# Unread float16 products among the first attention scores, and two groups of transfers written at other steps

## The chip, the cores and the metric

The kernel runs on one core of a Trainium2 chip. The metric is the device time of one execution in microseconds (us), taken as the median of several executions. Engines are named as in the profile: PE (TensorE) multiplies matrices, PEld is its weight load, DVE (VectorE) does elementwise work and reductions, ACT (ScalarE) evaluates functions and copies, POOL (GpSimd) works on the side, and SP (SyncE) starts nearly all transfers from one queue.

## The reference

Three layers run one after another on 3072 rows of 512 numbers.

- Attention: 4 batches, 8 heads, 768 positions, 64 numbers per head. A position sees the first `n_global` = 8 positions and the `n_local` = 96 positions up to itself, with a bias that falls with distance; then softmax and the product with `v`.
- A dense layer: `h = x @ w_in` (512 to 2048), `g = h if h > 0 else exp(h) - 1`, `y = g @ w_out` (2048 to 512).
- A routed layer: a row is kept as it is unless `x @ w_skip > 0`; the other rows go to the one of 8 experts with the largest gate logit, `out = x + gate * (relu(x @ w1[e]) @ w2[e])`.

```python
scores = scale * q @ k.T + bias; a = softmax(where(keep, scores, -1e9)); x = a @ v
h = x @ w_in; y = where(h > 0, h, exp(min(h, 0)) - 1) @ w_out
out[do_compute] = y + gate_w * (relu(y @ w1[e]) @ w2[e])
```

All inputs are float32. The kernel multiplies in float16 wherever it can, each operand split into a high and a low part, so that one product of the reference becomes three.

## The kernel before, in words

**Attention steps.** `att_step(t)` (line 350) handles one step: a tile `n` of 128 rows and one of its four pairs of heads. It issues the scores of step `t` (`att_scores`, line 239 on PE, line 248 on DVE, the exponential in line 253 on ACT), the preparation of the step before (`att_probs`, `att_turn`; line 293 is the transpose on PE) and the product with `v` of four steps back (`att_pv`, line 324). The first six tiles' scores, and everything of the first four tiles, are products of float32 operands; later tiles use float16 parts. Each pair of scores has one buffer per head (`s0`, `s1`), so the scores of a step wait until DVE has read those of the step before.

**Weights of the dense layer.** `w_load` (line 387) brings one sixteenth of both weight matrices (1 MB) into one of two buffers (`stage`). `w_prep` first gathers the number out of its bits in three passes over 1024 elements on DVE (lines 396, 397, 398), then splits it into float16 parts (line 404 on ACT, line 405 on DVE). `w_check` (line 416) reads the same 16 MB a second time, as tiles `wc`, and folds one word of each number into `andw`, for a test at the end whether the inputs suit the fast path.

**Dense steps.** `moe_h(m, f)` (line 428, 12 products of 384 columns, then lines 432 to 439 on ACT, DVE and POOL) and `moe_y(m, f)` (line 449, nine products of 512 columns), for eight blocks `m` of 384 rows and sixteen pieces `f`. The body of `program` first runs 16 attention steps (`4 * TB + LV`) with twelve halves of weight preparation between them, and then the 128 dense steps, with the remaining attention steps and, in block 0, the remaining weight preparation between them. `route_init` (line 453) loads the gate's weights and clears the table `xg` by 16 transfers of 257 KB out of one tile `zrow` (line 475); it stands at step 12 of block 0. The second reading starts at step 16 (`c = s_ - NF`). From the second block on, `route` sends the rows of the block before to their experts; the experts themselves follow at the end.

**What sets the order.** The order in which `program` issues instructions is not the order in which they stand on the engines. The framework schedules each engine's instructions by its own estimate of when they are ready, and lets an instruction that is ready early pass others. `pin` (line 72) takes an instruction out of that freedom: pinned instructions keep the order of the program among each other. Transfers started by SP stand in one queue in that scheduled order, and each waits there for what it needs while those behind it wait too. Two transfers into `stage` can be under way at once; the next one waits until a buffer has been read.

Of the kernel before, what the change touches and what calls it, by code (L numbers as in the profile page):

```python
# [9 lines left out]
F32 = DT.float32  # L10
# [9 lines left out]
P = 128  # L20
B, H, S, D = 4, 8, 768, 64
NT, DM, FF = 3072, 512, 2048
E, F2 = 8, 1024
NB = S // P
NTILE = NT // P
TB = 3
TN = TB * P
NM = NT // TN
NF = FF // P
ND = DM // P  # L30
CAP = 256
# [10 lines left out]
ROW = DM + 2  # L42
# [9 lines left out]
LP, LV = 1, 4  # L52
# [10 lines left out]
class Fast:  # L63
# [281 lines left out]
    def att_xturn(self):  # L345
        if self.xs:
            xT, xs = self.xs.pop(0)
            self.nc.sync.dma_start_transpose(xT, xs.rearrange("p s h d -> p (s h d)"))

    def att_step(self, t):  # L350

        n, hp = divmod(t, H // 2)
        last = 4 * NTILE
        if t < last:
            self.att_scores(t)
        if 0 <= t - LP < last:
            self.att_probs(t - LP)
        if 0 <= t - LV < last:
            g = t - LV
            m, c = divmod(g // 4, TB)  # L360
            if m not in self.xT:
                self.xT[m] = self.mp.tile([P, 2 * ND, TN], F16, tag="xT", name=f"xT_{m}", bufs=2)
            self.att_pv(g, self.xT[m], c * P)
        if n + 1 < NTILE:
            self.att_split(n + 1, hp)
        if hp != 3 or n >= NTILE:
            self.att_xturn()
        if 0 <= t - LP < last:
            self.att_turn(t - LP)
        if hp == 1 and n + 2 < NTILE:  # L370
            self.att_load(n + 2)
# [81 lines left out]
    def route_init(self):  # L453
        nc = self.nc
        self.wg = self.ct([P, ND, E + 1], F32, "wg")
        nc.sync.dma_start(self.wg[:, :, 0:E], self.a["moe2_w_gate"].rearrange("(c p) e -> p c e", p=P))
        nc.sync.dma_start(self.wg[:, :, E:E + 1], self.a["moe2_w_skip"].rearrange("(c p o) -> p c o", p=P, o=1))

        self.wgs = self.ct([P, ND, 2, E + 1], F16, "wgs")
        t = self.ct([P, ND, E + 1], F32, "wgt")  # L460
        nc.vector.tensor_scalar(t, self.wg, GS, None, ALU.mult)
        nc.vector.tensor_copy(self.wgs[:, :, 0, :], t)
        nc.vector.tensor_tensor(self.wgs[:, :, 1, :], t, self.wgs[:, :, 0, :], ALU.subtract)
        nc.vector.tensor_tensor(t, t, t, ALU.mult)
        self.wgm = self.ct([P, 2], F32, "wgm")
        nc.vector.tensor_reduce(out=self.wgm[:, 0:1], in_=t[:, :, 0:E], op=ALU.max, axis=AX.XY)
        nc.vector.tensor_reduce(out=self.wgm[:, 1:2], in_=t[:, :, E], op=ALU.max, axis=AX.X)
        self.esum = self.ct([P, TB], F32, "esum")
        nc.vector.memset(self.esum, 0.0)
        self.xg = self.dp.tile([E * CAP, ROW], F32, name="xg")  # L470
        z = self.mp.tile([P, ROW], F32, tag="yt", name="zrow", bufs=4)
        nc.gpsimd.memset(z[:, 0:DM + 1], 0.0)
        nc.gpsimd.memset(z[:, DM + 1:ROW], OOB)
        for n in range(E * CAP // P):
            nc.sync.dma_start(self.xg[n * P:(n + 1) * P, :], z)

    def route(self, m):

# [317 lines left out]
    def program(self, ep, wp, ap):  # L796
        tc, nc = self.tc, self.nc
        self.att_init(ap)
        self.counts()
        self.w_init(ep, wp)  # L800
        self.att_load(0, "q")
        self.consts()
        self.att_load(1, "q")
        self.w_load(0)
        self.att_load(0, "v")
        self.att_load(1, "v")
        self.w_load(1)
        self.gsum = self.ct([P, NM * NF], F32, "gsum")
        self.sqw = self.ct([P, 2], F32, "sqw")
        self.vf0 = self.raw[0]  # L810
        self.tables(ap)
        self.att_split(0, 1)
        done = [0]

        def whalf():
            if done[0] < 2 * NF:
                f, part = divmod(done[0], 2)
                self.w_prep(f, part)
                done[0] += 1
                if part == 0 and f + 2 < NF:  # L820
                    self.w_load(f + 2)

        t = 0
        while t < 4 * TB + LV:
            self.att_step(t)
            if t == 2:
                self.att_split(0, 3)
                self.maxsq(self.vf0[:, 0, :], self.sq[:, 2, 0:1])
            for _ in range(W_STEPS.count(t)):
                whalf()  # L830
            t += 1
        steps = [(m, f) for m in range(NM) for f in range(NF)]
        pend = []
        todo = [(e, k, j) for e in range(E) for k in range(8) for j in range(2)]
        self.nh, self.htags = 0, ("h",)

        def prep():
            if todo:
                e, k, j = todo.pop(0)
                if j == 0 and len(todo) > 4:  # L840
                    self.ex_load(*todo[3][0:2])
                self.ex_prep(e, k, j)

        for s_, (m, f) in enumerate(steps):
            if m < NM - 1:
                for _ in range(A_STEPS[min(m, 1)].count(f)):
                    self.att_step(t)
                    t += 1
            if m == NM - 1 and f == 0:
                ap.release()  # L850
                self.xp = tc.alloc_tile_pool(name="xp", bufs=2)
                self.esums = self.xp.tile([P, 32 * E], F32, tag="esums", name="esums", bufs=1)
                self.emax = self.xp.tile([P, 2 * E], F32, tag="emax", name="emax", bufs=1)
                nc.gpsimd.memset(self.esums, 0.0)
                for k in range(2):
                    self.ex_load(0, k)
            while done[0] < 2 * f + 2 and m == 0:
                whalf()
            self.moe_h(m, f)
            if m == NM - 1:  # L860
                for _ in range(EX_HALVES[f]):
                    prep()
            if m == 0:
                for _ in range(2):
                    whalf()
            if pend:
                pend.pop(0)()
            if m == NM - 1 and f in (11, 13):
                assert not pend
                for e in range(NX):  # L870
                    (self.ex_gather if f == 11 else self.ex_tokens)(e, 0)
            if s_ >= LAG:
                self.moe_y(*steps[s_ - LAG])
            if m == 0 and f == 12:
                self.route_init()
            c = s_ - NF
            if c == 0:
                self.w_load(0, "wc")
            if 0 < c <= 4 * NF and c % 2 == 0:
                self.w_check(*divmod(c // 2 - 1, 2))  # L880
            if f == LAG and m:
                pend = self.route(m - 1)
                pend.pop(0)()
        for k in range(LAG):
            self.moe_y(*steps[k - LAG])
        self.ex_tail(prep)
        wp.release()
        self.xp.release()
# [271 lines left out]
```

## Time and profile before

| | us |
|---|---|
| three timed executions | 887.74, 889.18, 889.23; median 889.18 |
| the profiled execution, timed | 886.45 |
| span of the profiled execution | 884.7 |
| PE busy / DVE busy / ACT busy | 825.5 / 608.3 / 535.7 |
| mean granted TensorE clock | 0.966 |

The span runs from the first to the last instruction. The granted clock is the share of 2.4 GHz that TensorE was given: 1.00 is 2.4 GHz, 0.50 is 1.2 GHz. A busy time of PE counts the modelled ends of pipelined products, so a busy PE is not one at its peak. In a list by time, a row gives the start, the time until the last of its instructions has ended, engine, line, what is written and read, and how many instructions; one float32 product is two instructions in the trace. What stands in brackets is idle time of the engine before the row, and what ended it.

### The profile page before, as it was taken

The numbers are of one execution on the slowest core, as the hardware profiler recorded it, in microseconds if no ns is written. First come the engines' busy times: TensorE is split into PE (matmuls) and PEld (weight loads), VectorE is DVE, ScalarE is ACT, GpSimd is POOL, SyncE is SP. The second block draws the span as 40 slices with busy tenths as digits, with TensorE's granted clock in tenths as the row PEclk, the third lists the DMA queues.
The fourth block names the chain that finished last, engine by engine and source line by source line (L and its number), as shares of the span: only waits on it lengthen the run. The fifth ranks groups of instructions, "written<-read, shape, count | busy, mean of one in ns | idle before, by whom it ended". The sixth has DMA issues, their size and how long they took to land.

```text
span 884.7 us, 17522 instructions
## 1 busy us (share of the span) xinstructions
PE 825.5 (93%) x6017; PEld 478.8 (54%) x6017; DVE 608.3 (69%) x2263; ACT 535.7 (61%) x1326; POOL 175.6 (20%) x201
## 2 busy tenths in 40 slices
PE   4999898989899999999999999999999889999895
PEld 2766444445455555555555555555554556766563
DVE  6876999768847756755764775672586967877532
ACT  4655677656667777777777677664665645655311
POOL 1000212211222322221232232223232111101010
PEclk9966999989899999999999999999999989999998
DMA  8878987999966536455544542531445778978510
GB/s 310 231 202 212 261 263 224 324 283 250 253 127 129 113 89 153 104 120 101 126 103 126 126 89 49 113 73 33 110 160 176 244 224 256 267 247 250 136 43 25
DMA packets 185394, 148.79 MB, mean 168 GB/s; under 512 B 152208, under 2 KB 154256, under 8 KB 181200
## 3 DMA queue, kind: packets, MB, share of 16 engines
q1 hardware_dynamic: 182096, 141.59, 61.6%
q0 software_dynamic: 3200, 5.99, 1.9%
q8 instruction: 49, 0.80, 0.4%
q14 instruction: 49, 0.40, 0.1%
HBM read 94.82 MB, written 21.08 MB: 131 GB/s over the span
## 4 chain that ended last, share of the span: by engine, by line
PE 63%; DVE 13%; issue 11%; DMA 10%; ACT 1%; POOL 1%; SPq 0%; POOLq 0%; DVEq 0%; ACTq 0%
PE h L428 23%; PE y L449 22%; PE s L239 6%; PE pv L324 6%; DMA out<-eres,ix 5%; PE eh L639 3%; PE eo L655 2%; DMA wc<-in_wf 2%; DVE wt L397 2%; DVE w L405 2%; DVE wt L398 1%; DVE p L248 1%; PE ptp L293 1%; DVE e L435 1%; DMA wr<-in_wf 1%
## 5 line engine op out<-in xcount | busy, mean ns | idle before, releaser
L428 PE MATMUL h<-xT,w 128*128 128x384 f16 x1536 | 277.3, 331 | 2.9 <-DVE e L435 2.8
L449 PE MATMUL y<-w,gs 128*128 128x512 f16 x1152 | 271.2, 379 | 2.6 <-ACT gs L438 1.8
L439 POOL TENSOR_TENSOR gs<-e,gs 128x384 f16<-128x384 f32 x128 | 127.3, 995 | 423.9 <-ACT gs L438 359.8
L428 PEld LDWEIGHTS <-w 128*128 128x128 f16 x1536 | 148.1, 99 | 106.7 <-issue 11.6
L449 PEld LDWEIGHTS <-gs 128*128 128x128 f16 x1152 | 109.9, 98 | 123.4 <-ACT gs L438 2.8
L435 DVE SCALAR_TENSOR_TENSOR e<-e,h 128x384 f32<-128x384 f32 x128 | 70.4, 551 | 80.2 <-ACT e L433 78.0
L438 ACT ACTIVATE gs<-e 128x384 f16<-128x384 f32 x128 | 66.8, 522 | 97.0 <-DVE e L435 96.4
L253 ACT ACTIVATE p<-p,st 128x232 f32<-128x232 f32 (+1 forms) x192 | 89.2, 465 | 43.4 <-DVE st L248 42.9
L639 PE MATMUL eh<-eyT,ew 128*128 128x128 f16 (+1 forms) x1152 | 101.8, 239 | 4.6 <-DMA eyT<-eyh 3.1
L655 PE MATMUL eo<-ew,ehs 128*128 128x512 f16 x384 | 100.7, 384 | 5.4 <-DVE ehs L643 5.4
L639 PEld LDWEIGHTS <-ew 128*128 128x128 f16 x1152 | 86.7, 99 | 30.8 <-issue 4.8
L603 DVE SCALAR_TENSOR_TENSOR ew<-er,ew 128x512 f16<-128x512 f32 x128 | 88.8, 712 | 9.9 <-ACT ew L602 8.9
L432 ACT ACTIVATE e<-h 128x384 f32<-128x384 f32 x128 | 61.3, 479 | 48.7 <-PE h L428 40.6
L641 ACT ACTIVATE ehs<-eh 128x128 f16<-128x128 f32 (+1 forms) x96 | 29.9, 312 | 95.9 <-PE eh L639 92.8
L248 DVE CUSTOM_DVE_ANT_0 p<-s,tab 128x232 f32<-128x232 f32 (+1 forms) x192 | 67.1, 376 | 26.9 <-PE s L239 25.3
L602 ACT ACTIVATE ew<-er 128x512 f16<-128x512 f32 x128 | 75.4, 619 | 4.2 <-DMA er<-in_moe_w 4.1
L283 DVE TENSOR_TENSOR ph<-p,ph 128x464 f16<-128x464 f32 x68 | 43.5, 653 | 36.5 <-ACT ph L282 36.5
L433 ACT ACTIVATE e<-e 128x384 f32<-128x384 f32 x128 | 66.5, 520 | 3.1
L239 PE MATMUL s<-qh 64*128 64x232 f16 (+1 forms) x432 | 40.7, 258 | 14.5 <-DVE st L248 14.0
L655 PEld LDWEIGHTS <-ehs 128*128 128x128 f16 x384 | 35.1, 99 | 31.3 <-DVE ehs L643 8.3
L643 DVE SCALAR_TENSOR_TENSOR ehs<-eh,ehs 128x128 f16<-128x128 f32 (+1 forms) x96 | 31.7, 331 | 25.8 <-ACT ehs L641 25.5
L239 PE MATMUL s<-qk 64*128 64x232 f32 (+1 forms) x96 | 31.0, 565 | 15.6 <-DVE st L248 8.0
(170 smaller groups left out, 913.4 us busy)
## 6 DMA issues: line engine op xcount, KB each, us to landing
er<-in_moe_w SPq DMA_DIRECT2D x64, 512.0 KB
wr<-in_wf SPq DMA_DIRECT2D x16, 1024.0 KB
wc<-in_wf SPq DMA_DIRECT2D x16, 1024.0 KB
qk<-in_qk SPq DMA_DIRECT2D x20, 720.0 KB
out<-yt SPq DMA_DIRECT2D x24, 256.0 KB
rawv<-in_vp SPq DMA_DIRECT2D x21, 256.0 KB
xg<-zrow SPq DMA_DIRECT2D x16, 257.0 KB
yg<-xg SPq DMA_DIRECT2D x16, 257.0 KB
```

What stands on the lines that cost most here:

```text
L239: nc.tensor.matmul(sp[j], q[r, hp, KW:], k[r, hp, KW - w:KW], start=(x == 0), stop=(x == len(mm) - 1))
L248: nc.vector.tensor_tensor_reduce(pw[:, j, :], sp[j], self.tab[:, h, :] if i else self.tab0[:, h, :], -0.125, 3e38, ALU.add, ALU.min, st[:, ...
L253: nc.scalar.activation(pw[:, j, :], pw[:, j, :], AF.Exp, bias=st[:, 0, h:h + 1], scale=-1.0, accum_out=st[:, 1, h:h + 1])
L428: nc.tensor.matmul(hps, wi[:, s_, c, :], xT[:, x * ND + c, :], start=(n == 0), stop=(n == 3 * ND - 1))
L435: nc.vector.scalar_tensor_tensor(g, e, -HS, hps, ALU.mult, ALU.max, accum_out=self.gsum[:, m * NF + f:m * NF + f + 1])
L438: nc.scalar.activation(gs[:, 0], g, AF.Copy)
L439: nc.gpsimd.tensor_tensor(gs[:, 1], g, gs[:, 0], ALU.subtract)
L449: nc.tensor.matmul(self.ys[m][t], gs[:, s_, t * P:(t + 1) * P], wo[:, x, :], start=(f == 0 and n == 0), stop=(f == NF - 1 and n == 2))
L602: self.pin(nc.scalar.activation(w[:, 0], r, AF.Copy, scale=sc))
L603: nc.vector.scalar_tensor_tensor(w[:, 1], r, sc, w[:, 0], ALU.mult, ALU.subtract, accum_out=self.esums[:, c:c + 1])
L639: nc.tensor.matmul(hps, l, r, start=(i == 0), stop=(i == len(mm) - 1))
L655: nc.tensor.matmul(self.eo[(e, t)], hs[:, s_, j * P:(j + 1) * P], self.ew[(e, 4 + f // 2, f % 2)][:, x, :], start=(f == 0 and n == 0), sto ...
```

## The change: products on PE, and two groups of transfers

The change adds products whose result nobody reads, `keep_warm`: 40 ahead of step 0 and 8 ahead of each of the steps 1 to 15, 160 in all, each 128 x 128 times 128 x 256 in float16 on the constant tile `tri`, pinned. They write tiles of the tag `acc`, which the dense layer's sums use later. The clearing of `xg` becomes a function of one transfer, called at the dense steps 8 to 23. `route_init` stands at step 7 of block 0 and no longer at step 12. The second reading of the weights starts at step 32 and no longer at step 16.

```diff
+    def keep_warm(self, t, n):
+        o = self.ps.tile([P, 2 * P], F32, tag="acc", name=f"warm_{t}", bufs=3)
+        for _ in range(n):
+            self.pin(self.nc.tensor.matmul(o, self.tri[:, 1, :], self.tri.rearrange("p a b -> p (a b)"),
+                                           start=True, stop=True))
...
     def att_step(self, t):
...
+        if t < 4 * TB + LV:
+            self.keep_warm(t, 8 if t else 40)
         if t < last:
             self.att_scores(t)
...
-        z = self.mp.tile([P, ROW], F32, tag="yt", name="zrow", bufs=4)
+        z = self.zrow = self.mp.tile([P, ROW], F32, tag="yt", name="zrow", bufs=4)
...
-        for n in range(E * CAP // P):
-            nc.sync.dma_start(self.xg[n * P:(n + 1) * P, :], z)
+    def clear(self, n):
+        self.nc.sync.dma_start(self.xg[n * P:(n + 1) * P, :], self.zrow)
...
-            if m == 0 and f == 12:
+            if m == 0 and f == 7:
                 self.route_init()
-            c = s_ - NF
+            if NF // 2 <= s_ < NF // 2 + E * CAP // P:
+                self.clear(s_ - NF // 2)
+            c = s_ - 2 * NF
             if c == 0:
                 self.w_load(0, "wc")
```

Lines after line 350 carry other numbers in the changed kernel: 396, 397, 398, 405, 435 and 387 become 405, 406, 407, 414, 444 and 396.

**The first place is PE ahead of the second scores.** `s` are scores, `qk` the tile of queries and keys, `ptp` a transpose, `warm` what the added products write. Before:

```order
L239 MATMUL s_0_165<-qk_96 128x128
L239 MATMUL s_0_166<-qk_96 128x128
L239 MATMUL s_1_174<-qk_96 128x128
L239 MATMUL s_1_175<-qk_96 128x128
L293 MATMUL ptp_183<-ident,p_169 128x128 x2
```

In the changed kernel, with each repeated pair of weight load and product shown once:

```order
L239 MATMUL s_0_206<-qk_96 128x128
L239 MATMUL s_0_207<-qk_96 128x128
L354 LDWEIGHTS tri
L354 MATMUL warm_164<-tri 128x256
L354 MATMUL warm_215<-tri 128x256
L239 MATMUL s_1_224<-qk_96 128x128
L239 MATMUL s_1_225<-qk_96 128x128
L293 MATMUL ptp_233<-ident,p_210 128x128 x2
L354 MATMUL warm_248<-tri 128x256
```

The first scores are not pinned and have passed the products: all 40 of step 0 and the 8 of step 1 stand between the scores of step 0 and those of step 1. After that there is a group of 8 in about every step, 14 groups in all, the last one ahead of the scores of step 15, and none between those and the first dense product, where the scores of steps 16 to 18 stand.

**The second place is DVE where the first dense step comes in.** `e` is the activation of a dense step, `w_0` and `w_1` are float16 weights, `wt` the gathered ones, `p` and `st` belong to scores, `vv` to values. Before:

```order
L283 TENSOR_TENSOR ph_75<-p_616,ph_75 128x2x232
L435 SCALAR_TENSOR_TENSOR e_0_648,gsum<-e_0_648,h_0_635 128x384
L405 SCALAR_TENSOR_TENSOR w_0_693<-wt_687,w_0_693 128x512
L405 SCALAR_TENSOR_TENSOR w_1_696<-wt_687,w_1_696 128x512
L212 SCALAR_TENSOR_TENSOR vv_714<-rawv_556,vv_714 128x8x64
L396 TENSOR_SCALAR wt_743<-wr_659 128x1024
```

In the changed kernel:

```order
L283 TENSOR_TENSOR ph_75<-p_792,ph_75 128x2x232
L414 SCALAR_TENSOR_TENSOR w_0_869<-wt_863,w_0_869 128x512
L414 SCALAR_TENSOR_TENSOR w_1_872<-wt_863,w_1_872 128x512
L212 SCALAR_TENSOR_TENSOR vv_890<-rawv_714,vv_890 128x8x64
L405 TENSOR_SCALAR wt_919<-wr_835 128x1024
L248 ISA p_988,st_787<-s_18_984,tab 128x232
L406 SCALAR_TENSOR_TENSOR wt_919<-wr_835,wt_919 128x1024
L248 ISA p_988,st_787<-s_18_985,tab 128x232
L444 SCALAR_TENSOR_TENSOR e_0_824,gsum<-e_0_824,h_0_811 128x384
```

Seven instructions with work of their own that stood behind the first activation now stand ahead of it.

**The third place is SP's queue where the second reading begins.** `wc` are the weights read again, `pT` and `xT` transposes by DMA. Before:

```order
L387 DMA wc_1753<-in_wf 128x2048
L301 DMA_TRANSPOSE pT_1254<-ph_77 128x8x128
L301 DMA_TRANSPOSE pT_1287<-pz_1269 128x4x128
L301 DMA_TRANSPOSE pT_1381<-pz_1364 128x4x128
L387 DMA wc_2053<-in_wf 128x2048
L301 DMA_TRANSPOSE pT_1486<-pz_1461 128x4x128
```

In the changed kernel:

```order
L396 DMA wc_2963<-in_wf 128x2048
L301 DMA_TRANSPOSE pT_1450<-ph_77 128x8x128
L301 DMA_TRANSPOSE pT_1483<-pz_1465 128x4x128
L301 DMA_TRANSPOSE pT_1579<-pz_1562 128x4x128
L396 DMA wc_3269<-in_wf 128x2048
L301 DMA_TRANSPOSE pT_1651<-pz_1626 128x4x128
```

Nothing has moved here: the second reading begins at the same place of the queue, since a load with a free buffer is taken early whatever step issues it. The 16 loads end at the same place of the queue too, and the 32 folds of line 416 lie on DVE between the activations of step 11 of block 0 and step 11 of block 1 in both kernels, some of them a few instructions apart. The 16 clearing transfers take nearly the same places. From step 12 of block 1 on, the order on all engines is the same in both.

## Rows read from the trace of the kernel before

**Rows 1.** The page: busy time by engine; the granted clock in 40 slices.

```profile
PE 825.5 (93%) x6017; PEld 478.8 (54%) x6017; DVE 608.3 (69%) x2263; ACT 535.7 (61%) x1326; POOL 175.6 (20%) x201
PEclk9966999989899999999999999999999989999998
```

**Rows 2.** Busy time by stretch: length, then engines, granted clock, DMA share, GB/s.

```profile
14.00:46.60 32.60, 32.06 (x120) 22.46 (x120) 28.07 (x78) 21.28 (x64) 1.21 (x8) 1.00 0.86 263
50.00:80.80 30.80, 30.15 (x116) 21.86 (x116) 19.46 (x49) 14.57 (x40) 0.28 (x2) 0.50 0.74 209
80.80:140.00 59.20, 52.41 (x345) 27.04 (x344) 56.78 (x110) 41.67 (x98) 12.67 (x10) 1.00 0.97 261
140.00:240.00 100.00, 87.13 (x608) 45.53 (x608) 81.86 (x277) 61.32 (x159) 22.31 (x22) 0.91 0.96 263
```

**Rows 3.** PE in order of time: float32 scores, transposes and products of the first steps.

```profile
24.20 1.15 PE L239 MATMUL s<-qk 64*128 64x232 f32 x4
25.27 1.11 PE L293 MATMUL ptp<-ident,p 128*128 128x128 f32 x4
...
35.66 5.22 PE L324 MATMUL pv<-vf,pTf 128*128 128x64 f32 x24
...
47.57 0.82 PE L293 MATMUL ptp<-ident,p 128*128 128x128 f32 x4
...
49.65 0.41 PE L293 MATMUL ptp<-ident,p 128*128 128x128 f32 x2 [0.49 <-issue]
...
61.10 1.15 PE L239 MATMUL s<-qk 64*128 64x232 f32 x4
...
78.21 7.28 PE L428 MATMUL h<-xT,w 128*128 128x384 f16 x36
...
102.40 0.66 PE L239 MATMUL s<-qk 64*128 64x232 f32 x4
```

**Rows 4.** Who DVE waited for from 14 to 84 us: total, times, longest.

```profile
DVE p L248 <- PE s L239: 9.7, 6, 2.7
DVE e L435 <- ACT e L433: 6.0, 1, 6.0
```

**Rows 5.** PE in order of time: the first two pairs of scores.

```profile
7.53 0.80 PE L239 MATMUL s<-qk 64*128 64x128 f32 x4 [7.53 <-DMA qk<-in_qk]
14.04 1.00 PE L239 MATMUL s<-qk 64*128 64x128 f32 x4 [5.72 <-DVE st L248]
```

**Rows 6.** Weight loads of float16 products at 79 us; twelve such products later, in the chain.

```profile
79.17 0.15 PEld L428 LDWEIGHTS <-w 128*128 128x128 f16 x1 [0.17 <-issue]
79.50 0.15 PEld L428 LDWEIGHTS <-w 128*128 128x128 f16 x1 [0.17 <-issue]
...
168.34 1.95 PE h L428 x12
```

**Rows 7.** Busy time by stretch, around a loss of the clock.

```profile
138.80:142.20 3.40, 0.86 (x9) 0.43 (x8) 3.40 (x12) 2.23 (x6) 0.00 (x0) 1.00 0.97 299
142.20:145.60 3.40, 3.04 (x14) 1.50 (x12) 3.40 (x12) 3.31 (x12) 1.86 (x2) 0.50 1.01 247
```

**Rows 8.** DVE from 14 to 80 us by line: busy time, mean ns of one, idle before.

```profile
L248 DVE CUSTOM_DVE_ANT_0 p<-s,tab 128x232 f32<-128x232 f32 (+1 forms) x35 | 12.2, 372 | 9.8 <-PE s L239 9.7
...
L405 DVE SCALAR_TENSOR_TENSOR w<-wt,w 128x512 f16<-128x512 f32 x14 | 9.5, 685 | 1.0 <-ACT w L404 1.0
L397 DVE SCALAR_TENSOR_TENSOR wt<-wr,wt 128x1024 int32<-128x1024 int32 x7 | 8.5, 1212 | 0.0
L396 DVE TENSOR_SCALAR wt<-wr 128x1024 int32<-128x1024 int32 x7 | 4.8, 689 | 0.3 <-DMA wr<-in_wf 0.3
```

**Rows 9.** The chain of waits: second readings; DVE's wait for them from 140 to 240 us.

```profile
154.49 7.07 DMA wc<-in_wf
...
213.88 7.15 DMA wc<-in_wf
...
DVE andw L416 <- DMA wc<-in_wf: 9.4, 6, 2.6
```

## The prediction

> **What bounds the kernel now.** I read the page first. PE is busy 93% of the span, and the slices of the clock dip early, in the third and fourth [rows 1]. So I went on to the busy time by stretch. From 50.0 to 80.8 us PE is busy 30.15 of 30.80 us at a granted clock of 0.50, which is 1.2 GHz, while DVE works 19.46 us of it [rows 2]. Here PE is the bound, at half speed. From 80.8 to 140 us it is DVE, with 56.78 of 59.20 us [rows 2]. A stretch after a DVE-bound one cannot start earlier unless DVE does, so what the change is worth is read from DVE's idle time before 80.8 us.
>
> The stretch from 14.0 to 46.6 us prints a clock of 1.00 [rows 2], and the durations say otherwise. Four score instructions take 1.15 us at 24.20 us, the same as at 61.10 us, where the clock is 0.50; at 102.40 us they take 0.66 [rows 3]. Four transposes take 1.11 us at 25.27 us and 0.82 us at 47.57 us [rows 3]. The clock was low from the first product to about 46.6 us, with nothing on record to print; it was high for the few microseconds until 50, and low again until 80.8. So the whole opening, up to the first dense product at 78.21 us [rows 3], runs at 1.2 GHz although PE hardly pauses (32.06 of 32.60 us [rows 2]). What ended the low clock at 80.8 us were the dense float16 products that began at 78.21 us.
>
> Last I read DVE's waits from 14 to 84 us: 9.7 us for scores of PE, and one wait of 6.0 us for the first dense activation [rows 4]. These 15.7 us are what a faster PE could give DVE back.
>
> **The change part by part.**
>
> *Price of a product.* It has 256 columns. Weight loads of float16 products with 384 columns follow each other by 0.33 us at the low clock, and twelve take 1.95 us at the full one [rows 6]. By columns that is 0.22 us and 0.108 us.
>
> *The opening.* All 48 products of steps 0 and 1 stand between the first two pairs of scores. The first pair ends at 8.33 us, the second begins at 14.04 us, freed by DVE [rows 5]. The gap of 5.7 us takes 48 products at the full clock (5.2 us: no cost), not 48 at the low one (10.6 us: 4.9 us late). The clock starts low and rose 2.6 us after the first dense product [rows 2, 3]. With 4 us low (18 products) and 30 at the full clock, 3.2 us, the second pair begins at about 15.5 us. I take 1.5 us lost, ends 0 and 4.9. Behind it wait DVE's first scores; DVE's weight preparation does not.
>
> *The steps.* A full step costs PE 1.07 us of scores, 1.05 us of transposes (differences of starts in [rows 3]) and 5.14 / 3 = 1.71 us of products with `v`, 3.83 us together. At the full clock the scores take 0.66 and the transposes 0.82 us [rows 3]; the products with `v` have no row in float32 at that clock, so they lie between 1.71 and half of it, and I take 0.86, because the scores nearly halve as well. That makes 2.34 us, and with eight products (0.87 us) 3.2 us. Now 18 steps take 64.2 us (14.04 to 78.21), 3.57 us each. DVE's share is 28.07 + 19.46 us, with 3.4 us between the two rows counted as full, 50.9 us or 2.83 us a step [rows 2]. So 14 steps with products go from 3.57 to 3.2 us, 5.2 us in all, and the four without from 3.57 to DVE's 2.83, 3.0 us. Of these 8.2 us I take 6.0, since PE and DVE would be nearly equal and wait for each other in turns. Ends: 2, if the clock is low for a part, and DVE's whole 9.7.
>
> *The first dense step.* DVE waits 6.0 us for it [rows 4], because its activation stands ahead of work that is ready. In the new order seven instructions come first: about 2 x 0.69 us (L405), as much as one of these for `vv`, 0.69 (L396), 1.21 (L397) and twice 0.37 + 0.08 (L248, and its read-out) [rows 8], 4.9 us. Its twelve products are also shorter: eight of them ran by 0.33 us until the clock rose at 80.8 us, 3.2 us for all, against 1.95 at the full clock [rows 6], 1.3 us less. I take back half of the wait, 3.0 us; ends 1.3 and 6.0. It is not more because the weights that two of the seven read must have landed by then.
>
> *The transfers that were to move.* The second reading is three times on the chain with some 7 us (the first and the last in [rows 9]), and DVE stands still 9.4 us for it [rows 9]. It would pay to move it. But it does not move: the queue takes a load as soon as a buffer is free, and in the built order the loads and the 32 folds stay where they were, apart from a few neighbours. The clearing is 16 transfers in both and keeps its places; the DVE work of `route_init` comes some instructions sooner and is the same. I cost all this at 0, with 3 us either way for neighbours that meet a load earlier or later. What hides the clearing is that nothing waits for it; without that cover each would be a 257 KB transfer ahead of a 1 MB weight load in the same queue.
>
> *The sum.* -1.5 + 6.0 + 3.0 = 7.5 us, against the profiled execution: 886.45 - 7.5 = 878.95 us. The median of the three runs, 889.18, is 2.73 us above it, and so I expect a median of **881.7 us**. After 240 us the order is the same and everything shifts as a block. About 0.2% (1.8 us) is what a measurement of this kernel can tell from no change.
>
> *A rule against the change.* PE was busy for 30.15 of 30.80 us, and the clock stayed at half [rows 2]. The Trainium skill, page "TensorE: Matmul & The Clock Gate", section "Why this matters for your kernels", says that keeping TensorE busy without a break gives the full clock and that only idle gaps take it away. The measurement decides against it: float32 products and transposes kept this PE busy and did not hold the clock. By the rule added products could only cost; that is the last rival.
>
> **The rivals.**
>
> *The clock falls back (slower).* Eight products are a quarter of a step. The clock fell at 50 us after float32 work with short pauses (0.49 us at 49.65 us [rows 3]), and at 142.2 us after a stretch with PE busy 0.86 of 3.40 us [rows 7]. At the low clock a step costs 3.83 + 1.74 = 5.6 us, on PE, which everything waits for. At the full one it costs 3.2. Against today's 3.57 us the change loses from the point where the clock is low in 15% of the steps. With half of the 14 steps low: 14 x (4.4 - 3.57) = 11.6 us, plus 1.5, minus 3.0 at the first dense step: 886.45 + 10.1, or 899 as a median. For it: the clock has been seen to fall within float32 work. Against it: the same work alone raised it once, at 46.6 us, so it does not lack much, and at a low clock the products themselves are 1.74 us of dense work a step.
>
> *Transfers take it back (no change).* From 80.8 to 240 us the transfer engines are busy 0.96 to 0.97 [rows 2]. If they, not DVE, set the pace there, DVE arrives earlier and waits longer for weights. Only the opening's loss stays, up to 1.5 us: 889 to 891. Against it: DVE waited 0.3 us for weights before 80 us [rows 8], and with shares of 0.86 and 0.74 there the transfers have 0.14 x 32.6 + 0.26 x 30.8 = 12.6 us to spare.
>
> *The shifted folds pay.* If the few folds that changed places meet loads that have landed, half of DVE's 9.4 us goes too: 7.5 + 4.7 = 12.2 us, 877.
>
> *The rule holds.* If something other than the kind of work sets the clock, the products change nothing about it and 112 of them cost 12.1 us on PE at 0.108 us, plus 1.5: 902.8.
>
> **How the numbers follow.** Forecast 0.60, clock falls back 0.15, transfers take it back 0.14, folds pay 0.07, rule holds 0.04. Faster by over 0.2%: 0.59 of the forecast, 0.07 of the folds, 0.03 of the transfers: 0.69. Within 0.2%: 0.01 and 0.08: 0.09. Slower: 0.15, 0.04 and 0.03: 0.22. The forecast's own range is 874 to 888 by the ends above taken in part. The range reaches to 891 for the transfers and to 873 for folds that pay more; outside lie the rule (0.04), most of the clock's rival (0.13) and 0.03 below.
>
> **What would show it.** Right: 160 products of line 354, the 112 later ones about 0.11 us apart; four score instructions in 0.66 us from 20 to 75 us; the wait of DVE for scores down from 9.7 to 4 us or less, the one for the first activation to about 3; the first dense product at about 72 us; the waits for `wc` as before. Wrong: a clock of 0.50 with products 0.22 us apart after 20 us, or a second dense block that starts no earlier although the first one did.

## The result and the profile after

The changed kernel takes 876.58 us (median of 4 runs, 872.5 to 877.69), the kernel before 889.2 us beside it. The ratio is 0.9841, with a 95% interval of 0.981 to 0.9872: 12.6 us faster between the medians (11.4 to 16.9 by the interval), where 7.5 were predicted. Its profiled execution took 877.69 us (span 876.0), the slowest of the four.

The page first: busy time and the granted clock in 40 slices. The third and fourth slices, 6 and 6 before [rows 1], read 9 and 8; PE is busy 7.0 us less, although it now does 160 products more.

```profile
PE 818.5 (93%) x6177; PEld 476.3 (54%) x6177; DVE 604.8 (69%) x2263; ACT 535.9 (61%) x1326; POOL 176.3 (20%) x201
PEclk9998899899999999999999999999999999999998
```

Then the same stretches as in [rows 2] (length; PE, PEld, DVE, ACT, POOL; granted clock, DMA share, GB/s).

```profile
14.00:46.60 32.60, 31.87 (x236) 23.88 (x233) 31.61 (x90) 24.48 (x74) 1.38 (x10) 1.00 0.96 283
50.00:80.80 30.80, 25.26 (x157) 16.60 (x157) 25.07 (x60) 20.74 (x56) 2.42 (x3) 0.89 0.99 267
80.80:140.00 59.20, 51.65 (x357) 27.20 (x355) 56.92 (x127) 40.11 (x97) 12.13 (x11) 0.94 0.92 237
140.00:240.00 100.00, 90.67 (x631) 47.42 (x630) 75.27 (x260) 63.24 (x157) 23.58 (x23) 0.95 0.98 268
```

The column to read is DVE's. In the first stretch it rises from 28.07 to 31.61 us of 32.60, in the second from 19.46 to 25.07. So DVE did 9.15 us more of its work in these two. In the first it is now nearly as full as PE (31.87). In the last stretch it has 6.6 us less left to do.

PE in order of time, as in [rows 3] and [rows 5]:

```profile
7.54 0.80 PE L239 MATMUL s<-qk 64*128 64x128 f32 x4 [7.54 <-DMA qk<-in_qk]
8.27 7.19 PE L354 MATMUL warm<-tri 128*128 128x256 f16 x48
15.39 0.49 PE L239 MATMUL s<-qk 64*128 64x128 f32 x4
...
34.67 2.79 PE L324 MATMUL pv<-vf,pTf 128*128 128x64 f32 x24
...
39.31 1.04 PE L354 MATMUL warm<-tri 128*128 128x256 f16 x8
40.28 0.66 PE L239 MATMUL s<-qk 64*128 64x232 f32 x4
40.88 0.66 PE L293 MATMUL ptp<-ident,p 128*128 128x128 f32 x4
41.37 1.04 PE L354 MATMUL warm<-tri 128*128 128x256 f16 x8
...
65.83 0.66 PE L239 MATMUL s<-qk 64*128 64x232 f32 x2 [1.67 <-DVE st L248]
70.10 5.66 PE L437 MATMUL h<-xT,w 128*128 128x384 f16 x24 [3.62 <-DMA xT<-xs]
```

Where nothing holds them, scores take 0.66 us from 20 us on (1.15 before), transposes 0.60 to 0.82 (1.11), and 24 products with `v` 2.79 us (5.22). The first dense product begins at 70.10 us instead of 78.21. The row also shows a wait that was not there before: PE stands idle 3.62 us for the transposing transfer of `xT`.

DVE's waits from 14 to 84 us [rows 4], and from 140 to 240 us [rows 9]; then the transfer of `xT` in the chain of waits (start, length):

```profile
DVE e L444 <- ACT e L442: 3.7, 1, 3.7
DVE p L248 <- PE s L239: 0.2, 1, 0.2
...
DVE andw L425 <- DMA wc<-in_wf: 11.3, 6, 6.0
```

```profile
61.08 8.88 DMA xT<-xs
```

The wait for scores is gone (9.7 to 0.2), the one for the first dense activation is smaller (6.0 to 3.7), and the one for the second reading of the weights is not: 11.3 us against 9.4.

To see where the gain arises, follow the start of the dense activation (the first `exp` of a step) through the program, in us:

| block, step | before | after | earlier by |
|---|---|---|---|
| 0, 0 | 81.6 | 73.8 | 7.8 |
| 0, 8 | 120.3 | 113.3 | 7.0 |
| 0, 12 | 146.5 | 136.2 | 10.3 |
| 1, 0 | 166.1 | 161.7 | 4.4 |
| 2, 0 | 254.9 | 243.0 | 11.9 |
| 7, 0 | 622.2 | 609.9 | 12.3 |

From block 2 on the two kernels run alike. Between blocks 0 and 2 the gain swings, because both kernels stand still there at different places. The last stretch, from block 7 to the end, took 262.5 us before and 266.1 after; in the other runs below, which leave its code as it is, it takes 264.3 to 271.1, so single profiles can't be compared through it. Nor is a few us in this table more than one profile against another: the run with the moves alone, below, begins block 7 at 617.9 us, 4.3 ahead of the kernel before, and its time can't be told from it.

### The profile page after: what moved, and what is told of

It is laid out like the page before. It is cut to its first block, busy times and chain, and to the rows that moved or that the text cites. A ratio compares the mean times of both kernels' runs of the same rounds, so it can differ in the third digit from the quotient of the medians.

```text
span 876.0 us, 17838 instructions
## 1 busy us (share of the span) xinstructions
PE 818.5 (93%) x6177; PEld 476.3 (54%) x6177; DVE 604.8 (69%) x2263; ACT 535.9 (61%) x1326; POOL 176.3 (20%) x201
## 4 chain that ended last, share of the span: by engine, by line
PE 61%; DMA 13%; DVE 12%; issue 11%; POOL 1%; ACT 1%; SPq 0%; POOLq 0%; DVEq 0%; ACTq 0%
PE h L437 23%; PE y L458 21%; PE s L239 5%; DMA out<-eres,ix 5%; PE pv L324 4%; PE eh L650 3%; PE eo L666 3%; DMA xg<-yt,pos 2%; PE warm L354 2%; DMA yTs<-yh 1%; DVE wt L406 1%; DVE wt L407 1%; DMA wc<-in_wf 1%; DVE e L444 1%; DVE w L414 1%
## 5 line engine op out<-in xcount | busy, mean ns | idle before, releaser
L447 ACT ACTIVATE gs<-e 128x384 f16<-128x384 f32 x128 | 66.9, 523 | 97.2 <-DVE e L444 96.3
L444 DVE SCALAR_TENSOR_TENSOR e<-e,h 128x384 f32<-128x384 f32 x128 | 70.5, 551 | 73.7 <-ACT e L442 71.0
L613 ACT ACTIVATE ew<-er 128x512 f16<-128x512 f32 x128 | 75.5, 620 | 6.7 <-DMA er<-in_moe_w 6.6
L239 PE MATMUL s<-qh 64*128 64x232 f16 (+1 forms) x432 | 40.9, 257 | 10.9 <-DVE st L248 8.4
L677 POOL DMA_INDIRECT out<-eres,ix x16 | 17.1, 1069 | 144.9 <-DVE eres L674 112.5
```

The costliest lines, as they stand in the source:

```text
L239: nc.tensor.matmul(sp[j], q[r, hp, KW:], k[r, hp, KW - w:KW], start=(x == 0), stop=(x == len(mm) - 1))
L444: nc.vector.scalar_tensor_tensor(g, e, -HS, hps, ALU.mult, ALU.max, accum_out=self.gsum[:, m * NF + f:m * NF + f + 1])
L447: nc.scalar.activation(gs[:, 0], g, AF.Copy)
L613: self.pin(nc.scalar.activation(w[:, 0], r, AF.Copy, scale=sc))
```

## The experiments

Two questions come first: whether the gain is the products' clock or the moved order, and whether the products would do the same without the clock. The first four runs share one set of runs of the kernel before, 887.45 us. Each ratio below is to the runs of before beside it.

**The moves without the products.**

```diff
-        if t < 4 * TB + LV:
-            self.keep_warm(t, 8 if t else 40)
```

> The changed kernel without its 160 products; clearing and second reading stay written where the change writes them. Theory A (the gain is the clock that the products hold up): no gain, 889 +- 3 us, clock 0.50 from 50 to 80 us, DVE's waits for scores before 84 us near 9.7 us. Rival B (the moved transfers and the shifted order bring it): 877 to 882 us. In between, 883 to 886, if each brings a part.

Measured: 886.08 us, ratio 0.9987 (0.9964 to 1.001), no difference that can be told. The scores at 61.50 us take 1.15 us for four, and DVE waits 9.7 us for them, as before. The moved calls brought nothing by themselves.

**The products without the moves.**

```diff
+    def keep_warm(self, t, n):
...
+        if t < 4 * TB + LV:
+            self.keep_warm(t, 8 if t else 40)
```

> The kernel before with the 160 products; clearing and second reading as before. Theory A: nearly the whole gain, 876 to 880 us, first dense product at 70 to 72 us, clock 1.00 until about 66 us. Rival B: 886 to 890 us.

Measured: 876.87 us, ratio 0.9896 (0.9863 to 0.9928). The first dense activation starts at 73.5 us and block 2 at 241.8, as in the changed kernel. The products bring the gain. By the ratios the changed kernel gains 0.55% more than this run; the two intervals overlap only from 0.9863 to 0.9872, so a small share that comes of both edits together is not excluded.

**The same order with products of 16 columns.**

```diff
-        o = self.ps.tile([P, 2 * P], F32, tag="acc", name=f"warm_{t}", bufs=3)
+        o = self.ps.tile([P, 16], F32, tag="acc", name=f"warm_{t}", bufs=3)
...
-            self.pin(self.nc.tensor.matmul(o, self.tri[:, 1, :], self.tri.rearrange("p a b -> p (a b)"),
+            self.pin(self.nc.tensor.matmul(o, self.tri[:, 1, :], self.tri[:, 1, 0:16],
```

> The changed kernel with products of 16 columns instead of 256: as many instructions in the program, pinned in the same way, with almost no work in them. Theory A: they do not hold the clock, so 0.50 through most of the opening and 889 to 896 us (they cost up to 0.077 us each at the low clock, twice what a product of 64 columns takes at the full one). Rival C (what helps is the order that the pinned products bring, not the clock): 877 to 882 us.

Measured: 892.55 us, ratio 1.0075 (1.0046 to 1.0103), slower than before. As many float16 instructions stand at about the same places, but the first rise of the clock on record is at 54.0 us, and it is half again from 57.4 to 88.2 us. PE in order of time shows float32 scores before 54.0 us as slow as in the kernel before:

```profile
24.50 0.41 PE L354 MATMUL warm<-tri 128*128 128x16 f16 x8
...
26.64 1.15 PE L239 MATMUL s<-qk 64*128 64x232 f32 x4
```

So neither the order that the products force nor a float16 instruction as such brings the gain. It comes with the clock; without it the run is slower than before.

**Products at the first two steps only.** This and the next three share a kernel before of 889.22 us.

```diff
-        if t < 4 * TB + LV:
+        if t < 2:
```

> The changed kernel with the unread products only at the first two steps (40 and 8), none in the twelve groups after them. Theory A (float32 scores, transposes and products do not hold the clock; the groups do): the granted clock rises near 12 us as in the changed kernel, is back at half before 25 us, and stays there until the first dense products at some 80 us; the first dense activation starts at 80 to 82 us instead of 73.8, and the time is 884 to 890 us, as without any product (886.08). Theory B (one push ahead of the first scores is enough, what follows holds itself up): the clock stays high to about 66 us, the steps lose the 12 x 8 products of 0.11 us, and the time is 872 to 877 us.

Measured: 885.2 us, ratio 0.9945 (0.9923 to 0.9968). The 48 products lift the clock at 12.1 us; it is half again from 18.9 us, but for 46.2 to 49.6 us, while PE is busy 32.22 of 32.60 us, nearly all of it float32 work. By stretch, in the columns of above:

```profile
14.00:46.60 32.60, 32.22 (x137) 22.89 (x135) 28.35 (x80) 21.76 (x65) 1.24 (x9) 0.58 0.93 268
50.00:80.80 30.80, 30.05 (x118) 21.77 (x117) 18.88 (x47) 14.49 (x39) 0.28 (x2) 0.51 0.75 207
```

This shows what the kernel before could only suggest: from 18.9 to 46.2 us the float32 scores, transposes and products do not hold the full clock that they were handed, and the twelve later groups carry most of the gain. Such work does not always lose it so soon. In the changed kernel the last unread product starts at 55.7 us, and the clock stays full to 66.6 us under float32 work alone. Type, shape (scores use 64 rows, products with `v` 64 columns) and pauses come together in this work, and no run separates them. The Trainium skill, page "TensorE: Matmul & The Clock Gate", section "Why this matters for your kernels", says that unbroken work on TensorE gives the full clock, and names idle gaps as what takes it away; it does not speak there of float32 against float16. These two rows differ from that, and the measurement decides.

**Four products a step instead of eight.**

```diff
-            self.keep_warm(t, 8 if t else 40)
+            self.keep_warm(t, 4 if t else 40)
```

> The changed kernel with groups of four products in each step instead of eight; the 40 ahead stay. Theory A (it is the clock that counts, and four products a step still hold it): clock high from 12 to 66 us; the half of the products that is left out lay beside VectorE, which is busy 31.6 of 32.6 us in these steps, so the time stays at 874 to 878 us. Theory B (four are too few): the clock falls back before 30 us, float32 scores take 1.3 us for four instructions instead of 0.66, the first dense activation starts at 79 to 82 us, and the time is 884 to 891 us. If the products themselves still cost something (theory C), the time falls to 870 to 873 us with the clock high.

Measured: 880.6 us, ratio 0.9894 (0.9863 to 0.9924). With four the clock is full from 12.9 to 67.5 us, nearly as with eight (11.9 to 66.6), and the first dense activation comes at 71.4 us, 2.4 earlier than with eight. But block 1 begins at 162.3 and block 2 at 244.3 us, later than with eight (161.7 and 243.0), with DVE waiting 13.5 us for `wc` after 84 us. The time came out just above theory A's 874 to 878; its interval touches that of the changed kernel. In this profile an early start of the dense work was lost within two blocks: that made the second reading, not the opening, the next thing to test.

**Products in four steps more.**

```diff
-        if t < 4 * TB + LV:
+        if t < 4 * TB + LV + 4:
```

> The changed kernel with groups of eight products in four steps more, up to the last steps of the first block. Theory A (the first dense products are held by the transposing transfer of xT, which stands in SP's queue behind the loads of qk and of the weights; the clock is secondary there): the first dense product still starts near 70 us; the clock is high through 66.6 to 73.4 us, where it was half, and the time changes by less than 2 us: 874 to 877.5 us. Theory B (the half clock at 66.6 to 73.4 us stands behind the late start): the first dense activation starts 1.5 to 3 us earlier than 73.8 and the time is 872 to 875 us. If the added products stand in the way of the last float32 work (theory C): 878 to 880 us.

Measured: 882.56 us, ratio 0.9905 (0.9871 to 0.9939). The run did not test what was meant: steps 16 to 19 are no longer ahead of the dense work but inside its first block, and the clock was half from 67.4 to 74.3 us as without them. The first of the four groups ran at 75.46 us, behind the first dense products, and the last ended at about 167 us, since their PSUM tiles come from the ring that the dense accumulators hold. It prices products placed among the dense work: slower, as in theory C, and somewhat worse than its 878 to 880.

**The second reading's loads held in program order.** In the changed kernel the call that starts the second reading stands at block 2, but the built order still takes the loads as buffers come free, from block 0 on. Here they are pinned (run with the first three, before 887.45 us).

```diff
-        self.nc.sync.dma_start(t, self.a["wf"].bitcast(I32)[f].rearrange("p k (d t) -> p k d t", t=2))
+        d = self.nc.sync.dma_start(t, self.a["wf"].bitcast(I32)[f].rearrange("p k (d t) -> p k d t", t=2))
+        if name == "wc":
+            self.pin(d)
```

> The changed kernel with the 16 loads of the second reading pinned as well, so that they stand where the change writes them; in the built order they then come later in the transfer queue (places 108 to 234 of its list, instead of 73 to 117). If the second reading's loads cost time in the first two dense blocks, as DVE's 11.3 us of waits for them say: 866 to 873 us, and no wait of DVE for them before 240 us. If other work paces those blocks anyway: 875 to 878 us.

Measured: 882.06 us, ratio 0.9941 (0.9914 to 0.9968), slower than without the pin. Block 2 began at 228.6 us, 14.4 earlier than in the changed kernel, and blocks 2 to 6 gave 22 us back (617.9 against 609.9 us at block 7). The loads were held but the folds that read them were not: they stood on DVE right behind the issue of their loads. From 84 to 500 us:

```profile
DVE andw L427 <- DMA wc<-in_wf: 25.4, 13, 3.5
```

**Loads and folds held.** As the run before, and:

```diff
-        self.nc.vector.scalar_tensor_tensor(self.andw, self.wc[:, k, :, 1], 0x40000000, self.andw,
-                                            ALU.bitwise_xor, ALU.bitwise_and)
+        self.pin(self.nc.vector.scalar_tensor_tensor(self.andw, self.wc[:, k, :, 1], 0x40000000, self.andw,
+                                                     ALU.bitwise_xor, ALU.bitwise_and))
```

> The changed kernel with the second reading of the weights really held back: the loads of wc and the folds that read them both keep their place in program order, where the run with the loads alone held had folds right behind their loads on VectorE and gave back 22 us in blocks 2 to 6. Theory A (the wait of VectorE for wc, and with it the stalls of blocks 0 and 1, are what the early second reading costs): no wait of VectorE for wc above 2 us in 84 to 500 us, block 2 starts at 226 to 231 us (243.0 in the changed kernel), a block stays at 73.5 to 75.5 us, and the time is 862 to 867 us. Theory B (what is saved early is paid late, since the 16 loads and folds only move into blocks that have no room for them): block 2 starts as early, but blocks 2 to 6 take 76 us or more and the time is 874 to 880 us.

Measured: 873.12 us, ratio 0.9807 (0.9772 to 0.9842). No wait for `wc` is left after 84 us, and block 1 runs without a stall. By stretch, to be held against the last row of the changed kernel above (PE 90.67, DVE 75.27):

```profile
140.00:240.00 100.00, 99.06 (x728) 53.04 (x727) 62.09 (x237) 71.72 (x179) 25.72 (x25) 1.00 0.59 135
```

Block 2 starts at 229.6 us, 13.4 earlier. Of that, 8.3 us are given back by block 7 (604.8 against 609.9). The time lies between the two theories, nearer to B, which had part of the saving paid back later: blocks 3, 4 and 5 take 76.6, 75.0 and 78.9 us, where the changed kernel takes 74.8, 73.7 and 74.8. There PE, which in the changed kernel is busy 230.14 of 230.50 us from 304 to 534.5, now waits for score statistics, and in three of the four waits a fold stands just ahead of them on DVE. These are 4.2 of the 7.2 us by which the three blocks are longer; the clock was also half there from 506.8 to 510.2 us.

```profile
PE s L239 <- DVE st L248: 4.2, 4, 1.8
```

**The folds where DVE is free.** The last three runs share a kernel before of 888.43 us. Dense steps 4, 5, 9, 10, 14 and 15 of a block carry no attention work.

```diff
-            c = s_ - 2 * NF
+            c = s_ - NF - 11
             if c == 0:
                 self.w_load(0, "wc")
-            if 0 < c <= 4 * NF and c % 2 == 0:
-                self.w_check(*divmod(c // 2 - 1, 2))
+            if c > 0 and f in (4, 5, 9, 10, 14, 15) and nfold < 2 * NF:
+                self.w_check(*divmod(nfold, 2))
+                nfold += 1
```

> As the run with loads and folds of the second reading held (873.12), but the folds stand only in the dense steps that carry no attention work (steps 4, 5, 9, 10, 14 and 15 of a block), from the end of block 1 to block 7, instead of in every second step of blocks 2 to 6. In that run TensorE waited 4.2 us in four pieces for the VectorE statistics of the scores between 304 and 534 us, with the folds on VectorE ahead of them, where the changed kernel shows no such wait. Theory A (it was the place of the folds): that wait is under 1 us, blocks 3 to 5 take 73.5 to 75 us each instead of 76.6, 75.0 and 78.9, and the time is 862 to 868 us. Theory B (it is the bytes, 512 KB to 1 MB more at a time beside the other transfers, wherever the folds stand): the blocks take 76 us as before and the time is 871 to 876 us.

Measured: 866.29 us (863.84 to 867.76), ratio 0.9737 (0.9675 to 0.9799): theory A, and the best version of this study. Its median is 10.3 us below that of the changed kernel (9.2 us by the ratios to before); the two intervals of the ratio don't overlap. Blocks 3 to 5 take 75.1, 74.0 and 75.5 us. PE waits for statistics 1.4 us from 302 to 526 us; under 1 was expected:

```profile
PE s L239 <- DVE st L248: 1.4, 3, 0.7
```

The edit also starts the folds five steps earlier and thins them from eight to six a block: they run from 219 to 595 us, where the run before had them from 240 to 536. So the place of the folds and their rate are not separated.

**That, with four products and the clearing held back.**

```diff
-            self.keep_warm(t, 8 if t else 40)
+            self.keep_warm(t, 4 if t else 40)
...
-        self.nc.sync.dma_start(self.xg[n * P:(n + 1) * P, :], self.zrow)
+        self.pin(self.nc.sync.dma_start(self.xg[n * P:(n + 1) * P, :], self.zrow))
```

> As the run with the folds in the free steps, with two edits more: four unread products a step instead of eight, and the clearing transfers held to their place in program order, so that none stands ahead of the first xT transfers. With four products the first dense activation came at 71.4 us instead of 73.8, but the 2.4 us were lost by block 2 among the waits for wc. Theory A (with the second reading out of the first blocks, what comes early stays early): first dense activation at 69 to 72 us, block 2 starts 2 to 4 us before the run with eight, and the time is 2 to 4 us below that run. Theory B (the first dense blocks are set by the first reading of the weights on VectorE and the transfers, not by when they begin): block 2 starts within 1 us of that run and the time is the same within 1.5 us.

Measured: 869.97 us, ratio 0.9793 (0.9729 to 0.9856), not to be told from the run before by the intervals, and above both theories' times. The new wait for `xT` is gone and the clock stays full to 81.4 us:

```profile
64.76 6.01 PE L439 MATMUL h<-xT,w 128*128 128x384 f16 x36
```

The first dense product is 5.3 us earlier than in the changed kernel, and the first dense activation, at 66.9 us, is 7.3 earlier than in the run before. But 0.9 us of that is left at block 1 and 1.8 at block 2. That is nearer to theory B: when the dense work begins hardly matters here. DVE, with the first reading of the weights, still has its work to do: 74.10 us of it in block 0, against 67.94 in the run before. So the new wait of 3.6 us probably costs little. At block 7 this run is still 1.6 us ahead, but its last stretch takes 271.1 us against 266.2, with the same code: in these two profiles it is the later stretch, not the opening, that makes the difference.

**The folds moved, without products.**

```diff
-        if t < 4 * TB + LV:
-            self.keep_warm(t, 8 if t else 40)
```

> As the run with the folds in the free steps, without any unread product. Theory A (clock of the first block and second reading are two separate costs that add): it is slower than the run with both by 9 to 13 us, as 886.08 against 876.58; that is 873 to 879 us with that run at 862 to 868. Theory B (the late second reading lets the first dense blocks catch up whatever the start, and the products then buy little): slower by under 5 us.

Measured: 881.85 us, ratio 0.9925 (0.9892 to 0.9957), 15.6 us above the run with the products. The products' gain is not used up by moving the folds: theory A rather than B, though both the difference and the time lie above its 9 to 13 and its 873 to 879 us. What the folds' place is worth without products is about 0.6% (0.9987 to 0.9925), and with them 1.1% (0.9841 to 0.9737), by ratios whose intervals are too wide to tell these two apart.

The pair also shows how the gain grows after the opening. The first dense activation is 8.4 us apart (74.2 and 82.6), block 1 is 14.2 us apart (152.7 and 166.9), with no second reading in block 0 in either. Over block 0 the DVE columns read:

```profile
74.20:152.70 78.50, 72.52 (x484) 38.11 (x483) 67.94 (x161) 56.96 (x140) 17.98 (x16) 0.97 0.72 189
```

```profile
82.60:166.90 84.30, 74.00 (x486) 38.46 (x485) 72.99 (x170) 59.30 (x145) 18.56 (x16) 0.98 0.75 188
```

With the products DVE has 5.05 us less to do in the block: it prepared more of the weights before, in the time in which it had waited for scores. The 30th of the 32 splits into float16 parts on DVE (line 405 of the kernel before) starts 12.6 us apart (124.4 and 137.0). It was 9.4 apart in the changed kernel and the one before (125.6 and 135.0).

## Why the prediction was right, and where its sizes were off

The direction and the mechanism held: the opening ran at half the clock, float16 work nobody reads lifts it, and what the change is worth is DVE's idle time before the dense blocks. By its steps:

- *The opening*, -1.5 us: the second pair of scores began at 15.39 us instead of 14.04, so -1.35. The 48 products lasted 7.19 us, as the sum of 4 + 3.2 us had it, and the clock rose 3.6 us after the first of them, at 11.9 us, where 4 had been allowed. The delay was right as one of PE. But DVE hardly waited for it (0.2 us for scores in all), so by the prediction's own measure it should not have been subtracted.
- *The steps*, +6.0 us with an end of 9.7: this term was mis-sized. The prediction took less than the whole because "PE and DVE would be nearly equal and wait for each other in turns". DVE's wait for scores went from 9.7 to 0.2 us, so +9.5, near the end of the range. Two things made it too small. The discount of 2.2 us failed: DVE did not wait in turn with PE, but worked 31.61 of 32.60 us. And a step of PE was priced too long, so that only 8.2 us stood there before the discount. The products with `v` were reckoned well (0.86 us, measured 2.79 / 3 = 0.93), but scores and transposes were taken at 0.66 and 0.82 us, to the end of their last instruction. By differences of starts, as at the low clock, they cost 0.60 and 0.49 (40.28 to 40.88 to 41.37 above), and eight products 0.97 (39.31 to 40.28): 2.99 us a step instead of 3.2, so that 14 x (3.57 - 2.99) + 3.0 = 11.1 us, more than DVE's whole 9.7.
- *The first dense step*, +3.0 us: the wait went from 6.0 to 3.7, so +2.3. The first dense product came at 70.10 us, where 72 was named, although PE waited 3.62 us for `xT`. That wait was not foreseen. It appears in the run with the products alone as well (2.54 us, in its first dense row). With four products a step it is 2.96 us, and two clearing transfers start ahead of `xT` within 2.1 us; with four products and the clearing held back it is gone. So it belongs to what the queue holds ahead of `xT` when the dense work comes early, the clearing above all.
- *The moved transfers*, 0 with 3 either way: right for the change as it stands. The moves alone gave a ratio of 0.9987, and the products alone 0.9896. The row to look for, the waits for `wc`, was 11.3 us against 9.4.
- *The sum.* -1.35 + 9.5 + 2.3 is 10.45 us, against 12.6 between the medians and 12.3 at the start of block 7. Of the 5.1 us that the forecast of 7.5 missed, 3.5 are the steps' term. DVE itself was busy 71.23 us up to 84 us instead of 60.18, 11.05 more: without the opening's 1.35 the sum comes nearer. The last 1 to 2 us are no more than single profiles differ by. They may lie in blocks 0 and 1: from 140 to 240 us PE waited 13.1 us for DVE's statistics before and 6.2 after, while the waits for `wc` grew by 1.9. Which of these stalls falls where changes with every version, and how much is owed to which was not separated.

The rivals: the clock did not fall back while groups stood in the steps. It fell at 66.6 us, as the gap ahead of the first dense product began (its last work ended at 66.49), 11 us after the start of the last unread product and just after a pause of 1.67 us; the prediction had no loss there. By stretch:

```profile
66.50:73.40 6.90, 3.30 (x11) 1.60 (x12) 4.09 (x9) 1.20 (x4) 0.00 (x0) 0.51 1.14 331
```

Without the later groups it fell at 18.9 us, 3.7 us after the start of the last product. So this rival named something that happens in this work, and that did not happen with eight or four products a step. *Transfers take it back* is refuted for the whole, though DVE's wait for `wc` did rise. *The shifted folds pay* named nearly the right time, 877, for a wrong reason: the waits for `wc` did not shrink, and the products without the shifted folds took the same 877. *The rule holds* fell with the result itself: 876.58 us, where it had 902.8.

What the prediction saw and left unpriced was the second gain: it said of the second reading: "It would pay to move it. But it does not move". Both halves were right. Once the loads and their folds were really held, and put where DVE is free, it was worth some 9 to 10 us more.

## What to carry to other kernels

When TensorE is nearly always busy, compare one kind of instruction at two places before calling it the bound: if four float32 scores take 1.15 us here and 0.66 there, the clock is half, and a few unread float16 products a step may cost less than the full clock gives back. Read the worth of it from the idle time of the engine that is the bound next, DVE here, not from the start of the stretch that follows: an early start was lost, early work was kept. And where a scheduler orders the queues, a call moved in the code may move nothing. Hold the transfer and what reads it together, in a place where the reading engine has room.

## What the runs showed that was not expected

- With four products a step the clock was full from 12.9 to 67.5 us, nearly as with eight; with groups of eight products of 16 columns it was half nearly throughout.
- A clock that had been lifted at 12.1 us was half again from 18.9 us under float32 work with PE busy 32.22 of 32.60 us; in the changed kernel it stayed full for 10.9 us behind the start of the last unread product, under the same kind of work.
- The printed clock is silent before its first event: the run without products prints 1.00 for 50 to 80.8 us, where four scores take 1.15 us, as at the granted 0.50. Durations, not that column, told the level there.
- Holding a transfer back without its reader made the kernel slower than leaving both alone (882.06 against 876.58 us), through DVE's 25.4 us of waits, although block 2 began 14.4 us earlier.
